# Splitting the last two heads' output product over PE's two column groups, with two copies on ScalarE

## Chip, cores and metric

One core of one Trainium2 chip. The metric is the device time of one execution in microseconds (us), the median of several runs; a profile is one execution, whose span is some 1.3 us shorter than its time. Engines: PE is TensorE (PEld its weight loads), ACT ScalarE, DVE VectorE, POOL GpSimd.

## The reference, cut to what matters

```python
# x: 2048 tokens x 640; 32 heads of 20; hidden width 1728
q, k, v   = split_heads(x @ wqkv)
phi_q     = concat(softmax(q @ w_phi), softmax(-(q @ w_phi)))    # 40 features a head; phi_k alike
kv, z     = phi_k^T v, sum_s phi_k                               # per head
a         = (phi_q kv / (phi_q z + 1e-6)) @ wo                   # <- this product
b         = (silu(x @ w_gate) * (x @ w_up)) @ w_down
out       = g * a + (1 - g) * b                                  # g = sigmoid(sum(x * gate_w))
```

The change touches phi_q kv for heads 30 and 31 alone.

## The kernel before

Tokens are handled in four blocks of 512. Features are packed in 11 chunks of three heads (120 rows), the last of two (80 rows). For each block, three work items (`O` parts 0, 1, 2) multiply a chunk of phi (transposed, `phiT`) by that chunk's `kvsb`; chunk j goes to PSUM partitions 0 to 63 if j is even and 64 to 127 if it is odd, so the two chunks of a pair sit in different column groups of PE. The eleventh chunk goes to partitions 64 to 103 and is copied into rows 64 to 103 of slice 13 of `hT`, where the down product finds it.

```python
def oitem(bt, part):
    buf = bt % 2
    pr = next_pair()                       # two PSUM banks, least recently used pair
    pairs = []
    for i, m in enumerate([2 * part, 2 * part + 1]):
        for s in range(2):
            j = 2 * m + s
            if j >= NCH: continue          # NCH = 11
            if j == NCH - 1:
                l, o = kvsb[0:80, j, 0:40], bank(2 * pr + i, 0, 512, 64, 104)
                r = phiT[0:80, buf, :, j, :]
            else:
                l, o = kvsb[0:120, j, :], bank(2 * pr + i, 0, 512, 64 * s, 64 * s + 64)
                r = phiT[0:120, buf, :, j, :]
            pairs.append((o, l, r, True, True, False))
    mm(pairs)
    if part < 2:
        copy("act", oT[:, buf, 2 * part:2 * part + 2, :], halves(pr, 512))
    else:
        copy("act", oT[:, buf, 4, :], bank(2 * pr, 0, 512))
        copy("act", hT[64:104, buf, 13, :], bank(2 * pr + 1, 0, 512, 64, 104))
# ... [cut] the order of items around the first block's O parts (Q: query projection, D: down product):
#   O0.0 O0.2 c4 B5 A6 O0.1 C5 c5 Q7 Q8 B6 C6 c6 D0.1 B7 Q9 D0.3 ...
```

A down product (`ditem`, `D`) waits at its head for all that it reads: every slice of `hT` and of `oT`, so also for the last of the `O` copies of its block.

The softmax here doesn't subtract the row's maximum and nothing guards it: scores larger than these inputs give would overflow.

## Time and profile before

| | before |
|---|---|
| time, median of the first three runs (range) | 288.96 us (288.51 to 289.04) |
| span of the profile | 287.3 us |
| PE busy | 284.5 us, 99% |
| ACT busy | 151.9 us, 53% |
| stretches of kvsb products (four, 11 matmuls each) | 1.423 or 1.424 us each (1.43 in the windows) |
| first stretch's first matmul, from the span's start | 125.996 us |
| from there to the start of the program's last matmul | 159.169 us |

In a line of the windows view the columns are the stretch, its length, then for each engine its busy time and number of instructions, the granted clock, the DMA share and GB/s. In the timeline they are start, length, engine, line, operation, output <- input, shape and count. All times given to a nanosecond below are read from single records of the trace.

### The profile page before, as it was taken

The numbers are of one execution on the slowest core, as the hardware profiler recorded it, in microseconds if no ns is written. First come the engines' busy times: TensorE is split into PE (matmuls) and PEld (weight loads), VectorE is DVE, ScalarE is ACT, GpSimd is POOL, SyncE is SP. The second block draws the span as 40 slices with busy tenths as digits, with TensorE's granted clock in tenths as the row PEclk, the third lists the DMA queues.
The fourth block names the chain that finished last, engine by engine and source line by source line (L and its number), as shares of the span: only waits on it lengthen the run. The fifth ranks groups of instructions, "written<-read, shape, count | busy, mean of one in ns | idle before, by whom it ended". The sixth has DMA issues, their size and how long they took to land.

```text
span 287.3 us, 4960 instructions
## 1 busy us (share of the span) xinstructions
PE 284.5 (99%) x1975; PEld 174.7 (61%) x1975; DVE 163.4 (57%) x243; ACT 151.9 (53%) x252; POOL 159.9 (56%) x125
## 2 busy tenths in 40 slices
PE   8999999999999999999999999999999999999997
PEld 7667777675644545557775556675554446656776
DVE  2337748576569978589991565970317899000000
ACT  0767778576775566682535653225586552234112
POOL 8286999879446789836542438350754558501000
PEclk9999999999999999999999999999999999999999
DMA  7975797000010598202573002061020006210101
GB/s 236 200 117 120 114 292 257 3 1 2 2 47 0 130 283 162 50 2 50 68 155 73 3 1 50 2 155 37 2 50 0 3 1 123 52 46 0 49 23 48
DMA packets 48944, 21.62 MB, mean 75 GB/s; under 512 B 39384, under 2 KB 48792, under 8 KB 48920
## 3 DMA queue, kind: packets, MB, share of 16 engines
q1 hardware_dynamic: 47400, 20.43, 31.2%
q10 hardware_dynamic: 1520, 0.87, 1.0%
q8 instruction: 16, 0.26, 0.4%
q14 instruction: 8, 0.07, 0.1%
HBM read 9.29 MB, written 2.62 MB: 41 GB/s over the span
## 4 chain that ended last, share of the span: by engine, by line
PE 99%; DVE 0%; issue 0%
PE ps L296 97%; PE ps L478 1%; PE ps L308 1%; DVE osb L733 0%
## 5 line engine op out<-in xcount | busy, mean ns | idle before, releaser
L324 POOL TENSOR_TENSOR hT<-hT,us 128x512 bf16<-128x512 bf16 (+1 forms) x56 | 65.1, 1175 | 65.3 <-DVE hT L328 47.0
L328 DVE SCALAR_TENSOR_TENSOR hT<-hT,ps 128x512 bf16<-128x512 bf16 (+1 forms) x56 | 37.4, 682 | 67.0 <-ACT hT L314 53.3
L296 PE MATMUL ps<-xT,wg 128*128 128x512 bf16 x260 | 64.6, 379 | 0.0
L296 PE MATMUL ps<-xT,wu 128*128 128x512 bf16 x260 | 64.6, 379 | 0.0
L296 PE MATMUL ps<-wd,hT 128*128 128x320 bf16 (+2 forms) x462 | 63.9, 295 | 0.0
L324 POOL TENSOR_TENSOR ph<-eq,qc 128x1320 bf16<-128x1320 bf16 x16 | 42.4, 2648 | 25.6 <-DVE qc L638 20.8
L296 PEld LDWEIGHTS ps<-wd,hT 128*128 128x128 bf16 x462 | 44.5, 98 | 17.4
L296 PE MATMUL ps<-wqk,xT 128*128 128x320 bf16 x320 | 47.7, 299 | 0.0
L314 ACT ACTIVATE hT<-ps 128x512 bf16<-128x512 f32 (+2 forms) x60 | 35.7, 596 | 16.7 <-PE ps L296 16.5
L296 PEld LDWEIGHTS ps<-xT,wu 128*128 128x128 bf16 x260 | 25.4, 98 | 30.7
L314 ACT ACTIVATE us<-ps 128x512 bf16<-128x512 f32 (+1 forms) x56 | 33.5, 598 | 19.2 <-PE ps L296 18.2
L314 ACT ACTIVATE osb<-ps,omg 128x640 bf16<-128x640 f32 (+2 forms) x17 | 12.9, 758 | 55.7 <-PE ps L296 55.7
L296 PEld LDWEIGHTS ps<-xT,wg 128*128 128x128 bf16 x260 | 25.0, 98 | 27.8 <-ACT oT L314 0.8
L324 POOL TENSOR_TENSOR ekr<-ekr,krec 128x1280 bf16<-128x1280 bf16 x16 | 37.4, 2358 | 5.8 <-DVE krec L338 5.8
L296 PEld LDWEIGHTS ps<-wqk,xT 128*128 128x128 bf16 x320 | 30.5, 98 | 13.1 <-issue 0.4
L314 ACT ACTIVATE eq<-ps 128x640 bf16<-128x640 f32 x32 | 22.4, 704 | 20.8 <-POOL ph L324 10.7
L335 DVE TENSOR_REDUCE ksum<-ekr 128x64 f32<-128x1280 bf16 x16 | 23.5, 1470 | 11.7 <-ACT ekr L314 11.7
L314 ACT ACTIVATE ekr<-ps 128x640 bf16<-128x640 f32 x32 | 22.3, 704 | 8.7 <-PE ps L296 8.2
L335 DVE TENSOR_REDUCE qz<-eq 128x64 f32<-128x1280 bf16 x16 | 23.7, 1478 | 2.6 <-ACT eq L314 2.6
L296 PE MATMUL ps<-wog,oT 128*128 128x320 bf16 (+2 forms) x165 | 24.7, 294 | 0.0
L296 PE MATMUL ps<-wvg,xT 128*128 128x320 bf16 (+1 forms) x160 | 24.1, 299 | 0.0
L335 DVE TENSOR_REDUCE qw<-ez 128x64 f32<-128x1280 bf16 x16 | 23.6, 1476 | 0.0
(73 smaller groups left out, 189.4 us busy)
## 6 DMA issues: line engine op xcount, KB each, us to landing
out_dram<-osb SPq DMA_DIRECT2D x15, 160.0 KB, 1.9
wd<-in_B_w_down_dram SPq DMA_DIRECT2D x1, 2080.0 KB, 9.6
wg<-in_B_w_gate_dram SPq DMA_DIRECT2D x1, 1040.0 KB, 10.6
wu<-in_B_w_up_dram SPq DMA_DIRECT2D x1, 1040.0 KB, 12.8
wg<-in_B_w_gate_dram SPq DMA_DIRECT2D x1, 800.0 KB, 5.8
wu<-in_B_w_up_dram SPq DMA_DIRECT2D x1, 800.0 KB, 8.3
wog<-in_A_wo_dram SPq DMA_DIRECT2D x2, 375.0 KB, 7.1
xs<-in_A_x_dram ACTq DMA_DIRECT2D x3, 160.0 KB, 3.6
```

Of the source, the lines that this page charges most:

```text
L296: last = pe.matmul(o, lhsT=l, rhs=r, start=st, stop=sp_, skip_group_check=sk)
L308: last = pe.transpose(o, i, ident[0:k, 0:k])
L314: return run("act", lambda: act.activation(o, i, func, scale=scale), rd, [o])
L324: return run(e, lambda: eo.tensor_tensor(o, a, b, op), [a, b], [o])
L328: return run("dve", lambda: dve.scalar_tensor_tensor(out=o, in0=a, scalar=s, in1=b, op0=op0, op1=op1), rd, [o])
L335: return run("dve", lambda: dve.tensor_reduce(o, i, AX.X, ALU.add), [i], [o])
L478: last = pe.matmul(bank(2 * pr, 0, P), lhsT=c, rhs=c, start=True, stop=True)
```

## The change

Intent: the eleventh product runs alone in the upper column group, while five products run in the lower and five more in the upper. Cut along the tokens, half of it goes to each group. Its results then lie on different partitions, so that two copies are needed.

```diff
                 if j == NCH - 1:
-                    l, o = kvsb[0:80, j, 0:40], bank(2 * pr + i, 0, 512, 64, 104)
-                    r = phiT[0:80, buf, :, j, :]
+                    for g, p0 in enumerate((0, 64)):
+                        pairs.append((bank(2 * pr + i, 256 * g, 256 * g + 256, p0, p0 + 40),
+                                      kvsb[0:80, j, 0:40], phiT[0:80, buf, 2 * g:2 * g + 2, j, :],
+                                      True, True, False))
+                    continue
@@
-            copy("act", hT[64:104, buf, 13, :], bank(2 * pr + 1, 0, 512, 64, 104))
+            copy("act", hT[64:104, buf, 13, 0:256], bank(2 * pr + 1, 0, 256, 0, 40))
+            copy("act", hT[64:104, buf, 13, 256:512], bank(2 * pr + 1, 256, 512, 64, 104))
```

## The prediction

> **What bounds the kernel now**
>
> I read the page first: the share of each engine, then the chain that ended last.
>
> ```profile
> span 287.3 us, 4960 instructions
> PE 284.5 (99%) x1975; PEld 174.7 (61%) x1975; DVE 163.4 (57%) x243; ACT 151.9 (53%) x252; POOL 159.9 (56%) x125
> ...
> PE 99%; DVE 0%; issue 0%
> PE ps L296 97%; PE ps L478 1%; PE ps L308 1%; DVE osb L733 0%
> ```
>
> TensorE (PE) is busy all through, and the last chain is PE and nothing else. So time that leaves PE's stream leaves the span, provided that PE doesn't then wait; time added to ScalarE (ACT, 53% busy) costs only where PE comes to wait for it. A busy share doesn't say how tightly PE is packed, so I looked next at the instructions that the change touches, which are those that read kvsb.
>
> ```profile
> L296 PEld LDWEIGHTS ps<-phiT,kvsb x44: 99/109/113, 126.0 to 256.6; 120*64 120x64 bf16 x40, 80*40 80x40 bf16 x4
> L296 PE MATMUL ps<-phiT,kvsb x44: 377/379/403, 126.0 to 256.8; 120*64 120x512 bf16 x40, 80*40 80x512 bf16 x4
> ```
>
> There are 44 of them, 11 for each of the four token blocks: ten for three heads each and one, 80*40, for the last two heads. That one is what the change splits. Each records some 379 ns, but matmuls are pipelined, so that is no price. The price is in the windows of the four stretches, from the first of the eleven to the matmul after the last, and in the timeline around the first stretch.
>
> ```profile
> 125.99:127.42 1.43, 1.43 (x12) 0.60 (x12) 1.43 (x2) 1.32 (x2) 0.58 (x1) 1.00 0.00 0
> 153.61:155.04 1.43, 1.43 (x13) 0.60 (x12) 0.00 (x0) 1.29 (x3) 0.00 (x0) 1.00 0.00 0
> 196.86:198.29 1.43, 1.43 (x13) 0.60 (x12) 0.00 (x0) 1.29 (x3) 0.00 (x0) 1.00 0.00 0
> 255.73:257.16 1.43, 1.43 (x13) 0.60 (x12) 0.00 (x0) 1.29 (x3) 0.00 (x0) 1.00 0.00 0
> ```
>
> ```profile
> 124.82 1.24 PE L296 MATMUL ps<-xT,wu 128*128 128x512 bf16 x5
> 126.00 1.49 PE L296 MATMUL ps<-phiT,kvsb 120*64 120x512 bf16 x11
> 127.42 2.89 PE L296 MATMUL ps<-wqk,xT 128*128 128x320 bf16 x20
> ```
>
> Five full-width matmuls of 512 columns take 1.24 us, so one follows another after (1.24 - 0.379) / 4 = 0.215 us. Eleven in single file would be 2.37 us; the stretch lasts 1.43. Six steps of 0.215 make 1.29, and the remaining 0.14 is the change of array form at the two ends and the slower first pair (403 against 379 ns). So the eleven run as five pairs and one alone: outputs on partitions 0 to 63 and 64 to 127 go through two column groups at once. By the program there are six for the upper group (the odd chunks and the last two heads) and five for the lower. The last-heads matmul is not itself alone: the trace starts it within 4 ns of a matmul of the next part, and it is the last matmul of the stretch, at 127.11, that has no partner. All four stretches have the same length to 0.01 us, so none of them waits for ACT today.
>
> **What the Trainium skill says**
>
> "TensorEngine Tiling (Array Packing)", Key Properties: tiles operate independently and matmuls on different tiles can run in parallel; changing the mode drains the array. The trace agrees: 1.43 us for eleven, with about 0.1 us between the stretch and its neighbours at either end. The change keeps the column mode, so adds no drain.
>
> "PSUM — Partial Sum Buffer", PSUM bank collisions: different column tiles may write the same bank at the same time if their partitions are disjoint. Today's pairs do just that, so the new halves (partitions 0 to 39 and 64 to 103 of one bank) should run together.
>
> "ScalarE: Activation LUTs", What ACT_TABLE_LOAD costs: an ACTIVATE with immediate operands takes 186 ns + 0.833 ns per column, and back-to-back ones overlap by about 93 ns. The slope agrees with the rows below; the overlap holds for most copies, but not around the copy of the last heads.
>
> ```profile
> L314 ACT ACTIVATE oT<-ps 128x1024 bf16<-128x1024 f32 x8 | 7.9, 1022 | 0.1
> L314 ACT ACTIVATE us<-ps 64x512 bf16<-64x512 f32 x4 | 2.4, 594 | 0.1
> L314 ACT ACTIVATE hT<-ps 40x512 bf16<-40x512 f32 x4 | 2.4, 592 | 0.1
> L314 ACT ACTIVATE oT<-ps 128x512 bf16<-128x512 f32 x4 | 2.4, 590 | 0.0
> ```
>
> **The change, part by part**
>
> PE. Per block one 512-column matmul goes and two of 256 columns come, one per group. The upper group then has five and a half steps, the lower five and a half: all paired, nothing alone at the end. The 20 projection matmuls of 320 columns give (2.89 - 0.30) / 19 = 0.136 us a step; with 0.215 at 512, a column costs 0.41 ns, and a 256-column step is an estimated 0.110 us. The stretch falls from six steps to five and a half: 0.215 - 0.110 = 0.105 us a block, 0.42 us in four. This half step is all there is to gain: it isn't 0.215, since the last heads' matmul already shares its slot.
>
> Weights. One more load per block, four in all. A load takes 109 ns and runs under the matmul before it; under a half matmul of 110 ns it just fits. I allow 0.01 us a block at most.
>
> ACT. One copy of 592 ns becomes two of 256 columns. From 590 ns at 512 columns and 1022 at 1024 the slope is 0.844 ns a column, so a half is 592 - 216 = 376 ns. The fixed part of about 160 ns is paid twice. Now the place in time, ACT's timeline in the first block:
>
> ```profile
> 126.66 1.51 ACT L314 ACTIVATE oT<-ps 128x1024 bf16<-128x1024 f32 x2
> 128.20 0.59 ACT L314 ACTIVATE hT<-ps 40x512 bf16<-40x512 f32 x1
> 128.81 1.02 ACT L314 ACTIVATE oT<-ps 128x1024 bf16<-128x1024 f32 x1
> ...
> 130.01 0.10 PEld L296 LDWEIGHTS ps<-wd,hT 128*128 128x128 bf16 x1
> ...
> 130.15 0.30 PE L296 MATMUL ps<-wd,hT 128*128 128x320 bf16 x1
> ```
>
> The copies run in single file from 126.66 to 129.83, and 0.61 us lie between the start of the last heads' copy and the next, 0.02 more than its length: no overlap there. Two halves at 0.376 + 0.024 take 0.80 in place of 0.61, so ACT's file ends 0.19 us later. The first half reads partitions 0 to 39 and writes 64 to 103; the copy of us, which moves 64 rows from the upper to the lower half, takes 594 ns as any other, so the shift should be free.
>
> Where PE meets ACT. In the first block the down product (wd with hT, and with oT further on) waits for the last copy of oT. That ends at 129.83; its first weight load starts at 130.01, so there is 0.18 us to spare. After the change the copy ends at 130.02, and PE wants to load at 129.90. Elsewhere in the trace a weight load started 0.055 us after the copy that released it (19.12 to 19.18) and its matmul 0.02 to 0.05 after that. So the matmul comes at 130.09 to 130.12, not at 130.15 - 0.105 = 130.04: the first block keeps some 0.04 of its 0.105 us.
>
> In the other three blocks the matmul after the stretch waits for an older copy (0.5 us to spare), and what needs the last-heads copy or later ones starts 1.1 us or more after them: 0.19 later on ACT and 0.105 earlier on PE fit in. These keep 0.105 each, and ACT's 0.57 us there are hidden.
>
> Sum: 3 x 0.105 + 0.04 = 0.355; if the halves cost ACT less, 0.42. I take 0.37 us: 288.96 - 0.37 = about 288.6 us, 0.13% faster.
>
> **The rivals**
>
> A wait for ACT eats the gain. If the cross-partition half were slower or the two halves 0.4 us longer together, the first block would lose 0.2 us against today, and the sum falls to about 0.1: 288.85. For it: the thin 0.18 us. Against: one block only, in the other three PE next needs these copies over a microsecond later.
>
> The halves don't pair, or the half matmul waits for its weights (109 ns under 110). Then each block has six steps again or a little more, and ACT's extra makes the first block worse: 289.0 to 289.1. For it: the tight fit, and four more instructions. Against: pairs into one bank run today, and the last product of the kernel steps 96-column matmuls far faster than this.
>
> The lone matmul was a whole step, and all of it goes: 4 x 0.215 = 0.86 us, 288.1. Against: 11 matmuls need 5.5 steps at the least with two groups.
>
> **Range and chances**
>
> All the rivals lie within 0.3% of the time before. The three runs of before spread over 0.53 us, more than the effect, so the range is mostly noise: 288.2 to 289.0. A change of 2% would be 5.8 us, more than the four stretches last in all (5.72). Within 2%: 0.985; slower by over 2%: 0.01; faster: 0.005.
>
> **What would show it right or wrong**
>
> Right: the four windows shrink from 1.43 to about 1.32 us each; eight matmuls 80*40 of 256 columns, twelve of kvsb a block; eight copies of 40x256 of some 376 ns; and a small hold of PE, below 0.1 us, ahead of the first down product after the first stretch and nowhere else. Wrong: windows still of 1.43 (no pairing or weights in the way); half copies well over 400 ns; new PE idle after the later stretches; or matmuls all packed as foreseen and a time that still doesn't move.

## The result, and the profile after

Six runs each, taken together: before 288.91 us (288.51 to 289.04), changed 288.28 us (288.14 to 288.85). The ratio is 0.9985, with a 95% interval of 0.9972 to 0.9997; it is the mean time of one kernel's fast runs over the mean of the other's of the same rounds, so not quite the ratio of these medians. So the change is 0.15% faster, some 0.43 us, with an interval of 0.09 to 0.81.

From the changed kernel's page, its span, shares and chain:

```profile
span 287.0 us, 4972 instructions
PE 284.1 (99%) x1979; PEld 174.5 (61%) x1979; DVE 163.3 (57%) x243; ACT 152.4 (53%) x256; POOL 159.8 (56%) x125
...
PE 99%; DVE 0%; issue 0%
```

PE still sets the end, with four instructions more and 0.4 us less. ACT has four more and is 0.5 us busier. Next, its kvsb matmuls and the windows of the same four stretches:

```profile
L296 PE MATMUL ps<-phiT,kvsb x48: 274/378/403, 126.0 to 256.5; 120*64 120x512 bf16 x40, 80*40 80x256 bf16 x8
```

```profile
126.04:127.36 1.32, 1.32 (x13) 0.59 (x13) 1.32 (x2) 1.21 (x2) 0.47 (x1) 1.00 0.00 0
153.64:154.95 1.32, 1.32 (x13) 0.58 (x13) 0.00 (x0) 1.21 (x2) 0.00 (x0) 1.00 0.00 0
196.78:198.10 1.32, 1.32 (x13) 0.58 (x13) 0.00 (x0) 1.21 (x2) 0.00 (x0) 1.00 0.00 0
255.54:256.86 1.32, 1.32 (x13) 0.58 (x13) 0.00 (x0) 1.21 (x2) 0.00 (x0) 1.00 0.00 0
```

Twelve matmuls of a stretch where there were eleven, and each stretch is 1.32 us long, not 1.42: the halves run as a pair. In single records the two halves start 3 ns apart and the next pair 0.113 or 0.114 us after them; the stretches are 0.106 or 0.107 us shorter. The gaps ahead of each stretch (0.093 us) and after it (0.095) are those of before: no drain was added.

Now ACT's groups and the timelines of ACT, PEld and PE in the first block:

```profile
L314 ACT ACTIVATE hT<-ps 40x256 bf16<-40x256 f32 x8 | 3.0, 378 | 0.2
```

```profile
126.70 1.51 ACT L314 ACTIVATE oT<-ps 128x1024 bf16<-128x1024 f32 x2
128.24 0.78 ACT L314 ACTIVATE hT<-ps 40x256 bf16<-40x256 f32 x2
129.05 1.02 ACT L314 ACTIVATE oT<-ps 128x1024 bf16<-128x1024 f32 x1
...
129.68 0.57 PE L296 MATMUL ps<-wqk,xT 128*128 128x320 bf16 x3
...
130.14 0.13 PEld L296 LDWEIGHTS ps<-wd,hT 128*128 128x128 bf16 x2 [0.23 <-issue]
...
130.17 0.30 PE L296 MATMUL ps<-wd,hT 128*128 128x320 bf16 x1
```

The two half copies are 376 and 379 ns long and fill 0.80 us of ACT's file where one copy filled 0.62. The last copy of oT ends at 130.070, 4.029 us after the stretch's first matmul (before: 3.841). The first weight load of the down product comes 0.069 us later, its matmul at 130.169, and PE's stream has a hole of 0.084 us ahead of it. Such a hole is in no other block. The view names no other engine for the weight load's wait ("issue"), so what held PE is for the experiments to show. PE's next matmul would have been due at 130.085: the first block gained 0.106 us and gave 0.084 back.

From the first stretch's first matmul to the last matmul the changed kernel takes 158.823 us, 0.346 less than before. The spans differ by 0.30, since in this profile the first stretch started 0.045 us later; that part has nothing to do with the change, as the control run shows.

### The profile page after: what moved, and what is told of

Its sections match the earlier page's. It is cut to its first block, busy times and chain, and to the rows that moved or that the text cites. A ratio compares the mean times of both kernels' runs of the same rounds, so it can differ in the third digit from the quotient of the medians.

```text
span 287.0 us, 4972 instructions
## 1 busy us (share of the span) xinstructions
PE 284.1 (99%) x1979; PEld 174.5 (61%) x1979; DVE 163.3 (57%) x243; ACT 152.4 (53%) x256; POOL 159.8 (56%) x125
## 4 chain that ended last, share of the span: by engine, by line
PE 99%; DVE 0%; issue 0%
PE ps L296 97%; PE ps L478 1%; PE ps L308 0%; DVE xT L320 0%; DVE osb L737 0%; DVE wvg L320 0%
## 5 line engine op out<-in xcount | busy, mean ns | idle before, releaser
L314 ACT ACTIVATE hT<-ps 128x512 bf16<-128x512 f32 (+2 forms) x64 | 36.4, 569 | 16.8 <-PE ps L296 16.5
```

The costliest lines, as they stand in the source:

```text
L314: return run("act", lambda: act.activation(o, i, func, scale=scale), rd, [o])
```

## The experiments

The theory: (1) a stretch is as long as the longer of two independent files of matmul steps (a file: one group's or engine's work, one piece after another), so the gain is half a step per block; (2) in the first block, and there alone, ACT's longer file holds PE (PE stands still until a copy ends), and only because PE also comes earlier. The rivals: smaller matmuls are cheaper anyway; the hold has another cause; ACT's time alone makes it.

All kernels gave correct results. Each kernel has one profile, and most were run only that once; a single run's time says little here, since the runs of one kernel spread over a microsecond. But the part of a profile that starts with the first stretch repeats to a few nanoseconds, so that part is compared:

| run | four stretches, us | first down product after the stretch's first matmul, us | first stretch to last matmul, us |
|---|---|---|---|
| before | 1.424 1.423 1.423 1.423 | 4.150 | 159.169 |
| changed | 1.318 1.316 1.317 1.316 | 4.128 | 158.823 |
| changed again (control) | 1.318 1.316 1.316 1.316 | 4.131 | 158.824 |
| halves in one group | 1.424 1.425 1.425 1.425 | 4.151 | 159.174 |
| other cuts | 1.318 1.370 1.366 1.419 | 4.126 | 159.029 |
| half copies only | 1.425 1.423 1.423 1.424 | 4.151 | 159.170 |
| quarter copies only | 1.425 1.423 1.423 1.424 | 4.151 | 159.170 |
| changed, quarter copies | 1.317 1.316 1.316 1.317 | 4.240 | 158.936 |
| changed, projection first | 1.319 1.316 1.315 1.317 | 5.404 (one projection later) | 158.743 |
| before, projection first | 1.424 1.422 1.422 1.423 | 5.509 (one projection later) | 159.170 |
| changed, VectorE half | 1.318 1.316 1.316 1.317 | 4.054 | 158.750 |

### Control: the changed kernel again

No edit.

> The changed kernel itself once more, as a control on the chip of the next three. From the first matmul of the first stretch to the last matmul of the program it should last 158.82 us as in its first profile (before: 159.17), with a gap of 0.08 us ahead of the first down product; whatever differs more between runs lies ahead of the first stretch. Ratio to before 0.998 to 0.999.

Measured: 288.66 us (288.23 to 288.84, six runs) against 289.12 (288.32 to 289.40, eleven runs) of before on the same chip; ratio 0.9985, interval 0.9972 to 0.9999. The profile's span is 287.6 us, 0.6 more than in the first one, but from the first stretch on it differs by 0.001 us. So the effect repeats, and the spread between runs arises ahead of the first stretch. The timelines of PE, first of the kernel before's profile, then of this one, show where:

```profile
5.08 0.99 PE L296 MATMUL ps<-wvg,xT 128*128 128x320 bf16 x6
```

```profile
5.16 1.56 PE L296 MATMUL ps<-wvg,xT 128*128 128x320 bf16 x6
```

The same six matmuls take 0.99 us in one and 1.56 in the other. In single records the steps are 0.136 us there and 0.267 here, nearly double, until about 6.4 us into the span. Of the eleven profiles, six have two to six such steps (of 0.238 us or more), and there the first stretch starts at 126.249 to 126.761 us. Five have none. In four of these (before, changed, and the two runs told below with quarter copies in the changed kernel and with VectorE) it starts at 125.996 to 126.041 us. In the fifth, with quarter copies only, it starts at 126.240 us: PE fell behind by 0.09 us at 7.6 us and by 0.17 at 13.3, and no run tells why. So the double steps go with most of the spread, not with all of it. The Trainium skill, "TensorE: Matmul & The Clock Gate", What's actually happening, says that PE starts at half its clock, and that its release hangs on a window which runs freely and so varies from run to run. The doubled steps agree. The clock column of the profile reads 1.00 in those microseconds, but it can't tell: six of the eleven traces hold a record of the clock, and it begins only about where the steps shorten (4.81 us in the kernel before, 5.86 in the one with half copies only); the control's trace holds none.

### Both halves in one column group

```diff
-                    for g, p0 in enumerate((0, 64)):
+                    for g, p0 in enumerate((64, 64)):
@@
-            copy("act", hT[64:104, buf, 13, 0:256], bank(2 * pr + 1, 0, 256, 0, 40))
-            copy("act", hT[64:104, buf, 13, 256:512], bank(2 * pr + 1, 256, 512, 64, 104))
+            copy("act", hT[64:104, buf, 13, :], bank(2 * pr + 1, 0, 512, 64, 104))
```

> The last heads' product is cut into two halves of 256 columns, but both go to the upper column group (partitions 64 to 103), and one copy of 512 columns takes them out. Theory (the gain is the half step that the second group takes over): the upper group again has six steps, so each of the four stretches lasts 1.42 to 1.44 us as before, perhaps 0.01 more for the extra instruction, and the span is that of before within 0.1 us. Rival (smaller matmuls are cheaper by themselves, whichever group they go to): the stretches last some 1.32 us as in the changed kernel.

Its windows, of which one line:

```profile
154.26:155.69 1.43, 1.43 (x13) 0.70 (x13) 0.00 (x0) 1.29 (x3) 0.00 (x0) 1.00 0.00 0
```

As many instructions of the same sizes as in the changed kernel, and the stretch is as long as before; from the first stretch on it takes 0.005 us more. So the halving gives nothing; the second column group gives all.

### Other cuts, one in each block

```diff
+    LOW = (2, 1, 3, 4)            # lower group's share of four 128-token tiles, by block
@@
-                    for g, p0 in enumerate((0, 64)):
-                        pairs.append((bank(2 * pr + i, 256 * g, 256 * g + 256, p0, p0 + 40),
-                                      kvsb[0:80, j, 0:40], phiT[0:80, buf, 2 * g:2 * g + 2, j, :],
-                                      True, True, False))
+                    n = LOW[bt]
+                    for a, b, p0 in ((0, n, 0), (n, 4, 64)):
+                        if a < b:
+                            pairs.append((bank(2 * pr + i, P * a, P * b, p0, p0 + 40),
+                                          kvsb[0:80, j, 0:40], phiT[0:80, buf, a:b, j, :],
+                                          True, True, False))
   ... the copies are cut alike
```

> The changed kernel with another cut in each block: the lower group gets 256, 128, 384 and 512 of the 512 columns in blocks 0, 1, 2, 3, the upper group the rest. Theory (two independent files of steps, the longer one sets the stretch; five whole steps of the other heads in each): the longer file has 5.5, 5.75, 5.75 and 6 steps, so the stretches last 1.32, 1.37, 1.37 and 1.43 us, within 0.015 us. Rival (what counts is only that the product is cut and paired at all, or each pair is in lockstep with its partner and the groups don't run ahead of each other): blocks 1 and 2 show the same as block 0, or 1.43 and more.

```profile
126.76:128.08 1.32, 1.32 (x13) 0.59 (x13) 1.32 (x2) 1.21 (x2) 0.47 (x1) 1.00 0.00 0
154.35:155.72 1.37, 1.37 (x13) 0.84 (x13) 0.00 (x0) 1.26 (x2) 0.00 (x0) 1.00 0.00 0
197.55:198.92 1.37, 1.37 (x13) 0.83 (x13) 0.00 (x0) 1.26 (x2) 0.00 (x0) 1.00 0.00 0
256.36:257.78 1.42, 1.42 (x12) 0.59 (x12) 0.00 (x0) 1.29 (x3) 0.00 (x0) 1.00 0.00 0
```

Cuts of 256, 128, 384 and 512 columns give 1.318, 1.370, 1.366 and 1.419 us, each within 0.011 of the expectation. In the second and third block a group has a quarter step more to do than with the even cut, and the stretch is a quarter step longer. One group runs ahead of the other: in the second block's records, after the cut product, the matmuls of one group start 0.110 to 0.112 us ahead of the other's (0.300 and 0.410 us after the stretch's first matmul, and so to the end). The longer file sets the length: part (1) of the theory stands, and the even cut is the best of the four.

The same records settle a rival that the prediction named, that a half matmul has to wait for the next weights. The matmul after a piece of 128 columns starts 0.060 us after it, while the weight loads beside it are recorded with 0.112 us and end later than that. So the loads did not set the steps here.

### The copies alone, in halves

The kernel before, with

```diff
-            copy("act", hT[64:104, buf, 13, :], bank(2 * pr + 1, 0, 512, 64, 104))
+            for g in range(2):
+                copy("act", hT[64:104, buf, 13, 256 * g:256 * g + 256],
+                     bank(2 * pr + 1, 256 * g, 256 * g + 256, 64, 104))
```

> The product is that of before, one matmul of 512 columns; only its copy is cut into two of 256 columns on ScalarE. Theory (a hold of PE comes only from both parts together): ScalarE's file in the first block ends 0.19 us later, at about 0.19 us after that of before counted from the stretch's first matmul, PE's first down product is released about 0.07 us after it and starts within 0.03 us of where it started in the kernel before (4.15 us after the stretch's first matmul); the four stretches stay at 1.42 to 1.44 us; span as before within 0.1 us. Rival (the half copies are dear by themselves, or PE is held by something else that the change brings): the down product starts 0.08 us or more later than in the kernel before, or other places of PE show new idle time.

PE was not held (4.151 us), but the test was too mild: the second copy started 0.285 us after the first, not 0.400 as in the changed kernel, and ACT's file grew by 0.06 us in place of 0.19. Here the two copies overlapped; those of the changed kernel, which read different partitions, did not.

### The copies alone, in quarters

As the run before, with four pieces of 128 columns.

> The two half copies of the run without the halved product overlapped (0.285 us from one to the next[...]), so ScalarE's file grew by 0.06 us only, not by the 0.19 us that the change adds: that run was too mild. Here the product is that of before and its copy is cut into four pieces of 128 columns, which by the pieces seen so far (0.174 us from one to the next on the same partitions, 0.28 for the last) take 0.80 us in place of 0.62: 0.19 more, the same as the change. Theory (0.18 us of room before the weight load, used up only because PE also comes 0.105 us earlier): no gap, the first down product 4.15 us after the stretch's first matmul, 159.17 us from there to the last matmul, both within 0.01. Rival (ScalarE's 0.19 us alone hold PE): a gap of 0.05 us or more, 4.2 us and 159.22 us or more.

ACT's timeline, the weight load and the down product:

```profile
128.44 0.76 ACT L314 ACTIVATE hT<-ps 40x128 bf16<-40x128 f32 x4
129.23 1.02 ACT L314 ACTIVATE oT<-ps 128x1024 bf16<-128x1024 f32 x1
...
130.32 0.17 PEld L296 LDWEIGHTS ps<-wd,hT 128*128 128x128 bf16 x2
...
130.39 0.30 PE L296 MATMUL ps<-wd,hT 128*128 128x320 bf16 x1
```

ACT's last copy ended 4.009 us after the stretch's first matmul, 0.168 later than before. The weight load came 0.070 us after its end, 0.06 later than it would otherwise have, yet its matmul came on time, 4.151 us after the first. So 0.168 us more on ACT, nearly the 0.188 that the change adds, cost nothing while PE kept its old pace. The hold needs both parts.

### The changed kernel with more copies

```diff
-            copy("act", hT[64:104, buf, 13, 0:256], bank(2 * pr + 1, 0, 256, 0, 40))
-            copy("act", hT[64:104, buf, 13, 256:512], bank(2 * pr + 1, 256, 512, 64, 104))
+            for g in range(4):
+                p0 = 64 * (g // 2)
+                copy("act", hT[64:104, buf, 13, P * g:P * g + P],
+                     bank(2 * pr + 1, P * g, P * g + P, p0, p0 + 40))
```

> The changed kernel with each half copied out in two pieces of 128 columns, four copies on ScalarE in all. A piece should last 0.27 us and start 0.29 us after the one before, so the four take 1.17 us in place of 0.80. Theory (ScalarE's added time reaches PE one to one in the first block, and is hidden in the other three, which have a microsecond): the gap ahead of the first down product grows from 0.084 to some 0.45 us, no new gap elsewhere, 159.19 us from the first stretch's first matmul to the last matmul, so that the whole gain is gone. Rival (the hold has another cause): the gap stays near 0.08 us. Rival (the other blocks have less room than I think): gaps in them too, and over 159.3 us.

```profile
128.22 0.89 ACT L314 ACTIVATE hT<-ps 40x128 bf16<-40x128 f32 x4
129.13 1.02 ACT L314 ACTIVATE oT<-ps 128x1024 bf16<-128x1024 f32 x1
...
130.22 0.13 PEld L296 LDWEIGHTS ps<-wd,hT 128*128 128x128 bf16 x2 [0.34 <-issue]
...
129.65 0.57 PE L296 MATMUL ps<-wqk,xT 128*128 128x320 bf16 x3
130.25 0.30 PE L296 MATMUL ps<-wd,hT 128*128 128x320 bf16 x1
```

The size was a miss, the mechanism not. Pieces on the same partitions overlapped (0.174 and 0.178 us from one to the next), so the four filled 0.915 us, not 1.17. That is 0.112 more than the two halves (0.803), and the hole ahead of the down product grew from 0.084 to 0.196: by 0.112, one to one. No other block shows a hole. Of the gain 159.169 - 158.936 = 0.233 us are left.

### Other work for PE during the copies

One query projection moved ahead of the first down product:

```diff
- ... Q7 Q8 B6 C6 c6 D0.1 B7 Q9 D0.3 ...
+ ... Q7 Q8 B6 C6 c6 Q9 D0.1 B7 D0.3 ...
```

> The changed kernel, with one query projection (20 matmuls, 2.7 us of PE work counted by steps: half of it per bank pair) issued ahead of the first down product in place of behind it, so that PE has other work while ScalarE ends its copies. Theory (the hold of 0.084 us is ScalarE's last copy and nothing else): the gap ahead of the first down product vanishes, nothing else moves, the span falls by about 0.08 us against the changed kernel, to 286.9 us in a profile, and the time is 0.17 to 0.2% below that of before (about 288.35 to 288.45 for 288.9). Rival (PE is held there by another cause, or the projection waits for the same copy): the gap stays at 0.05 us or more, now ahead of the projection, and the span stays at 287.0 us.

(The projection is ten matmuls of 0.136 us, 1.36 us, not the 20 and 2.7 us that I wrote.) Of PE's timeline:

```profile
127.71 4.10 PE L296 MATMUL ps<-wqk,xT 128*128 128x320 bf16 x29
131.65 0.57 PE L296 MATMUL ps<-wd,hT 128*128 128x320 bf16 x3
```

29 steps of 0.136 from 127.71 end at 131.65, where the down product starts: no hole. From the first stretch on it takes 158.743 us, 0.080 less than the changed kernel and 0.426 less than before, which is four times 0.106. In time 288.31 us (288.11 to 288.84, six runs) against 289.27 (288.37 to 289.61, eleven runs) of before on that chip: ratio 0.9972, interval 0.9957 to 0.9988. I had expected 0.9980 to 0.9983, and a span of 286.9; it was 287.1, with a first stretch 0.21 us later than in the changed kernel's first profile. The timed runs can't tell this kernel from the changed one, for 0.08 us is far inside their spread; the profiles can.

The same move in the kernel before, as a check of the order itself:

> The kernel before with the one query projection ahead of the first down product. Theory (moving it only removes the hold, and before has none): 159.17 us from the first stretch's first matmul to the last matmul, within 0.01 of before. Rival (the new order is better or worse by itself): it differs by 0.03 us or more, and then the 0.080 us that the same move gained in the changed kernel are not all the hold.

It took 159.170 us from the first stretch on, as before to 0.001. The order is worth nothing by itself; the 0.080 us are the hold.

### VectorE copies the second half

```diff
-            copy("act", hT[64:104, buf, 13, 256:512], bank(2 * pr + 1, 256, 512, 64, 104))
+            copy("dve", hT[64:104, buf, 13, 256:512], bank(2 * pr + 1, 256, 512, 64, 104))
```

> The changed kernel, but VectorE copies out the second half. ScalarE's file in the first block then is 0.21 us shorter than before, VectorE gets the copy behind the chain that it works on until some 3.4 us after the first stretch's first matmul. Theory (PE is held by ScalarE's file alone): no gap ahead of the first down product, 158.74 us from the first stretch's first matmul to the last matmul. Rival (VectorE, being busy there, holds PE in its place): the gap stays or grows, or another wait of PE appears in one of the other blocks.

DVE's timeline:

```profile
129.50 0.43 DVE L320 CAST hT<-ps 40x256 bf16<-40x256 f32 x1
129.95 2.69 DVE L324 TENSOR_TENSOR ez<-eq,zb 128x1280 bf16<-128x1280 bf16 x1
```

The hole is gone but for 0.01 us (4.054 where 4.044 is due), and from the first stretch on it takes 158.750 us. The last 0.01 us may be VectorE's: its copy ended at 129.923 us, later than ACT's last one, and the weight load came 0.115 us after it. So it is as good as the moved projection, with an unwelcome neighbour: VectorE's next multiply took 2.69 us in place of 0.82, while POOL worked on ph. PE did not wait for it here. It ended 0.68 us after ph, which had started first and took 2.42 us; in the kernel before, the multiply started first, and ph took 2.94. The two traces look as if the two operations took turns; no run tests that.

## Why the prediction was right

It held: 288.6 us against 288.28, inside the range, and "within 2%" at 0.985. By itself that says little: the range was mostly noise, the old time of 288.96 lies in it too, and no rival reached 2%. What bears the prediction out is the profiles. By its steps:

- **PE bounds the kernel, all stretches are tight.** Right: what left PE's stream left the time, but for the hold.
- **Half a step per block, 0.105 us.** Right: 0.106 or 0.107. The step of 256 columns, estimated at 0.110, was 0.113, but the whole steps that ended the old stretches were longer too, 0.2195 us in place of 0.215 (two steps of the upper group in the first stretch, 126.671 to 127.110). The single group and the other cuts show that it is the second column group.
- **Weights just fit.** Right in outcome: no later pair was late, and the 0.01 us allowed was not needed. But the fit of 109 under 110 ns was not what decided: a matmul came 0.060 us after a quarter product, under loads of 0.112.
- **ACT's file 0.19 us longer.** Right: 0.188, from half copies of 376 and 379 ns that do not overlap. The shift of partitions was free in a copy's own length, as foreseen, but not in the file: two halves from the same partitions fill 0.675 us, these 0.803. By an estimate from these two and the release below, copies that overlapped would have let the weight load start 3.97 us after the stretch's first matmul and the down product at 4.00, ahead of the 4.044 at which PE is ready: no hold.
- **The first block keeps 0.04 us of its 0.105.** Right in kind, a little off in size: it kept 0.022 (0.019 in the control). The term was the release: 0.055 us from the copy's end to the weight load was read from one other place, where the copy was VectorE's (wqk, ended at 19.123 us) and not ACT's; here it was 0.069, and the matmul came 0.030 after it.
- **The other three hide ACT's time.** Right, even with 0.11 us more of it.
- **Sum 0.355 us, taken as 0.37.** Measured 0.346 within the profiles. The timed difference of 0.43 us agrees with it within its interval. That the medians differ by 0.63 us, more than the profiles account for, is taken as luck of the starts: over the eleven profiles the first stretch's start spreads by 0.77 us.

Of the rivals, the wait for ACT is there, at 0.084 us; the unpaired halves and the whole step did not come about.

## What to carry to other kernels

With two column groups, count the steps in each group's file; here the lone product's step was half hidden already, so cutting it evenly between files of six and five steps gained half a step, not a whole one. A gain on a full engine is kept only as far as its next wait has room: list the waits just behind the change with their slack, and where one is thin, put independent work ahead of it. When run-to-run spread is larger than the effect, compare the part of the traces behind the spread.

## What the Trainium skill lacked or had wrong

- "ScalarE: Activation LUTs", What ACT_TABLE_LOAD costs, gives an overlap of some 93 ns for back-to-back ACTIVATEs. That held for the pieces on the same partitions (379 ns long, the next 285 ns after), but not where the start partition of input or output changed from one to the next: these came 23 to 25 ns after the other's end in all cases that I looked at, which made the two half copies fill 0.803 us, against 0.675 for two halves on the same partitions. The changed kernel with quarter copies shows both in one file: all four pieces write from the same partition, and only between the second and the third, where the input's start partition changes, is there a gap (24 ns). Whether the partition itself counts or its shift from input to output, no run separates. It is not the only cause of such gaps: the two exponentials of one tile (eq<-ps and ekr<-ps, 704 ns each), both over all 128 partitions, also follow with 0.03 us between them in all 32 tiles' pairs of the changed kernel.
- "TensorEngine Tiling (Array Packing)", Key Properties, says that a change of mode drains, without a price: here 0.093 us ahead of the stretch, 0.095 after it and a first step 0.024 us longer. It says that tiles operate independently, but not how far: with the uneven cuts one group kept some 0.11 us ahead of the other to the end of the stretch, which lasted 1.370 and 1.366 us against 1.318.
- No page that I read gives the time from an ACTIVATE's end to a weight load that waits for it: 0.069 and 0.070 us, and 0.030 more to the matmul where PE stood still.
